# A fused attention, mixture of experts and gated layer on one core: the tokens' numbers scattered at a later place, the constants and the attention in another order

## The chip, the cores and the metric

The kernel runs on one core of a Trainium2 chip. Its engines are PE (TensorE, matrix products), DVE (VectorE), ACT (ScalarE), POOL (GpSimd) and SP (SyncE, which here only issues DMAs). Each engine works through its own list of instructions in order; a semaphore makes an instruction wait for another engine or for a DMA. The metric is the time of one execution on the device in microseconds, and the lower is the better.

## The reference

Three layers follow one another. Attention with a memory term over B=2, H=8, S=576, D=64, then a top-1 mixture of 8 experts with a capacity of 288 tokens, then a gated layer of width 1536, all in float32:

```python
scores = np.where(causal, -1e9, scale * q @ k.T); a = softmax(scores); local = a @ v
mem_out = (phi(q) @ M_prev) / (phi(q) @ z_prev + 1e-6)        # phi(x) = where(x > 0, x, exp(x) - 1) + 1
x = g * mem_out + (1 - g) * local                              # 1152 tokens of 512
expert_idx = argmax(x @ w_gate); gate_w = softmax(x @ w_gate)[expert_idx]
# the first 288 tokens of each expert are kept, in the order of the tokens
y[e] = relu(x[e] @ w1[e]) @ w2[e];  out[i] = gate_w[i] * y[expert of i, place of i]   # 0 where not kept
result = ((out @ w_a) * (out @ w_b)) @ w_out
```

## The kernel before

**Attention.** The 16 heads make 8 pairs, n = 0 to 7, four to a batch. A pair's 576 rows are cut into five tiles; a tile of a pair is a unit. Per pair, q and k are loaded by SP, turned by PE, split into a high and a low part by ACT and DVE, and POOL and SP place copies of these parts side by side: POOL makes copies in `d` and `qz`, and SP issues two DMAs `d<-s` (`side_by_side`, L495, the issue is L500), without which the pair's scores can't start. Per unit, PE makes the scores (L579), DVE the masked minima, ACT the exponentials, PE turns them and multiplies by v. Per pair, POOL makes phi(q) (L475, L481), and PE multiplies it by the memory (L522).

**Gate.** As tiles of tokens become whole, PE turns them and multiplies by `w_gate` (L730, 8 columns), DVE finds each token's expert, its probability and its place. `gate5` (L816) then has POOL issue an indirect DMA that scatters 128 tokens of 512 numbers into a DRAM buffer `xs_d`, sorted by experts; there are ten of them, five for each batch. `rank` (L854) sorts the experts by their number of tokens; it and `gate4b` (L788, the places of the last three tiles) run on DVE at the attention's end.

**Zeros.** `init_dram` (L407) has SP write zeros into `xs_d` and into the output, in ten parts between the attention's other issues. Its part 0 also writes `far`, a number that means none, into the 1152 words of `id_d`, a DRAM buffer with one 4-byte number to a row. The zeros come from a tile that shares its memory with the tile h, so these DMAs are printed as `xs_d<-h` and `out_dram<-h`.

**Experts and the gated layer.** Each float32 weight is split into a high and a low part by ACT (L961) and DVE (L964), or by integer operations on DVE (L1353 to L1363) with ACT's help (L1349), and each product is made of three matmuls (L949 to L951). Weights come from DRAM in blocks of 1 MB into a few buffers (`raw`, `raws`, `rawd`), issued by SP (L935 for the experts, L972 for the gated layer) as soon as a buffer is free. PE turns the tokens of an expert (L958) and uses L1539 for one kind of expert product.

**Tokens' numbers.** The last layer's results are written back by an indirect scatter which needs, for each row in the sorted order, the number of its token. `token_ids` (L898) makes them: four DVE instructions (L899 to L902) give every token's place `dsi`, and ten indirect DMAs of POOL (L808, by `scatter`) write the tokens' numbers `tid` into `id_d`, each 128 words of 4 bytes; a tile of 64 rows writes 64. Afterwards POOL loads all of `id_d` into the tile `ids`. The first use of `ids` is the first scatter of the output.

**What sets the order.** Nothing in the list of an engine is sorted by hand. `Plan` (L111) is a list scheduler: every piece of work has an engine, a cost, what it comes after, the buffers that it takes, and a key. It takes the work that can start first and, among those that can start within a share `AHEAD_` of the cost, the one with the smallest key; the keys are the pair's or unit's number plus an offset from the table `KEYS`. A call of `there` tells the plan when a load is expected. A piece of work's costs and due times only decide the order in which instructions are written, never a wait on the chip. The class `Way` (L1277) plans the experts and the gated layer in the same manner, with keys in the unit of expected time.

Of the kernel before, what the change touches and what calls it, by code (L numbers as in the profile page):

```python
# [21 lines left out]
SVB = 3  # L22
KEYS = dict(E=-210.8, E_=-463.7, F=981.4, F_=15.6, L=-19.8, M=23.3, M_=-352.9, N=429.9, N_=-217.9, O=185.9, O_=61.1,
            P=293, P_=-109.5, S=-8.9, S_=374.1, T=-187.5, T_=-396.9, V=-472.6, V_=432.7, X=-6.7, X_=-271.4, cv=-185,
            d=-57.5, e1=-507.1, e2=213.4, ec=894.9, eh=-120.4, ep=-803.9, ex=-13.3, ey=107.1, g1=-624, g1_=436.1,
            g1b=25.7, g1b_=19, g2=-336.8, g2_=216.5, g2b=186.5, g2b_=-486.8, g3=71.5, g3_=-527.6, g4=-221.2,
            g4_=157.3, g4b=209.7, g4b_=-689.3, g5=6, ge=68.8, ge_=125, gw=407.6, gw_=-144.8, kh=-415.4, kl=-145,
            kt=-27.5, mm=-190.6, mm_=40.1, mn=45.7, mo=217.3, mo_=-200.5, pb=-229.7, pw=-257.8, px=-331.6, qd=-154.1,
            qe=38.2, qh=-186.8, ql=237.9, qm=-200.6, qp=-217.5, qr=630.5, qt=-193.9, tc=-222.5, tot=279.3, tr=0.6,
            w=280.2, w_=-166)  # L30
GK = 0.0
AHEAD_ = 0.094
CHANGE = 0.25
# [3 lines left out]
ZS = 1  # L37
STIR = [16, 0, 16, 0]
GROUPS = [(0, 2), (2, 5)]
# [157 lines left out]
def fused_kernel(  # L197
# [125 lines left out]
    if STACK:  # L323
        mask2 = ap1.tile([128, S], F32, name="mask2")
        nc.gpsimd.memset(mask2, 0.0)
        for h in range(2):
            nc.gpsimd.affine_select(out=mask2[64 * h:64 * h + 64], in_=mask2[64 * h:64 * h + 64], pattern=[[-1, S]],
                                    base=NF_ * 128, channel_multiplier=1, compare_op=ALU.is_ge, fill=BIG)


        qd = [ap1.tile([128, 128], F32R, name=f"qd{n}") for n in range(3)]
        for t in qd:
            nc.gpsimd.memset(t.bitcast(F32), 0.0)
    for n in (1, 0):
# [7 lines left out]
    for t in range(2):  # L342
        nc.scalar.dma_start(out=zr[:, t, :], in_=z_prev.rearrange("b h d -> (b h) d"))
    Mp = M_prev.rearrange("b (p t) d e -> t d (b p) e", t=2)
    for t in range(2):
        nc.sync.dma_start(out=mb[64 * t:64 * t + 64, :, 64 * t:64 * t + 64], in_=Mp[t])

    bet = cst.tile([128, H], F32, name="bet")
    nc.scalar.dma_start(out=bet, in_=beta.rearrange("(o h) -> o h", o=1).to_broadcast([128, H]))
    load(0, "v")  # L350
    load(1)
    rg = cst.tile([128, H], F32, name="rg")
    rog = cst.tile([128, H], F32, name="rog")
# [32 lines left out]
    def gate_constants():  # L386
        nc.gpsimd.affine_select(out=tri, in_=ones, pattern=[[1, 128]], base=-1, channel_multiplier=-1,
                                compare_op=ALU.is_ge, fill=0.0)
        nc.gpsimd.iota(up, pattern=[[1, E]], base=0, channel_multiplier=0, allow_small_or_imprecise_dtypes=True)
        for p in range(E):  # L390
            nc.gpsimd.memset(prm[:, p:p + 1], float(RANKS[p]))
            nc.gpsimd.memset(lim[:, p:p + 1], float(LIMITS[p]))
        nc.gpsimd.iota(rev, pattern=[[-1, E]], base=E, channel_multiplier=0, allow_small_or_imprecise_dtypes=True)
        nc.gpsimd.affine_select(out=low, in_=ones[:, 0:E * E].rearrange("p (a b) -> p a b", a=E),
                                pattern=[[1, E], [-1, E]], base=-1, channel_multiplier=0,
                                compare_op=ALU.is_ge, fill=0.0)
        for b in range(B):
            nc.gpsimd.iota(tid[:, b * NT:b * NT + NT], pattern=[[128, NT]], base=b * S, channel_multiplier=1)
        for t in (oh, lgs, accs, gvm, pos, over, zero):
            nc.gpsimd.memset(t, 0.0)  # L400
# [601 lines left out]
    def dve_(c):  # L1002
        return 0.07 + 1.05e-3 * c

    for n in range(min(2, len(pairs))):
        for j, w in enumerate("qkv"):
            there(("load", n, w), [(w, (w, n))], (4.5, 5.5, 10.0, 11.0, 12.0, 13.0)[3 * n + j])
    there("d0", [("d", ("d", 0))])
    there("zr", late=9.0)
    work("small", "PE", 0.2, small_constants, ["zr"], (-6, None), [("C", "small")], late=0.4)  # L1010
    ZP = 10
    for n, (b, p) in enumerate(pairs):
        at_ = n * UP
        if n > 1:
            for w in "qkv":
# [9 lines left out]
             [("qT", n), ("s", n)])  # L1025
        work(("qd", n), "POOL", 1.1, lambda n=n: q_stack(n), [("ql", n)], (at_, "qd"), [("qd", ("qd", n))], [("s", n)])
        work(("qm", n), "POOL", 1.616, lambda n=n: q_min(n), [("qe", n)], (at_, "qm"), (), [("eq", n)])
        work(("qp", n), "POOL", 1.45, lambda n=n: q_phi(n), [("qm", n), ("qr", n)], (at_, "qp"), (),
# [7 lines left out]
        if n:  # L1036
            work(("dq", n), "POOL", 2.75, lambda n=n: q_beside(n), [("qh", n)], (at_, "d"), [("d", ("d", n))], [("s", n)])
            work(("dk", n), "POOL", 1.36, lambda n=n: k_beside(n), [("kh", n), ("dq", n)], (at_, "d"), (),
# [9 lines left out]
        for i in UNITS:  # L1048
# [6 lines left out]
            for h in range(1 if one else 2):  # L1055
                work(("M", u, h), "DVE", dve_(W), lambda u=u, h=h: minima(u, h), [("S", u)], (at_, "M"),
                     [("sv", ("sv", u, h))], [u])
# [32 lines left out]
    for z in range(ZP):  # L1090
        work(("z", z), "SP", 2.2, lambda z=z: init_dram(z, ZP), [("S", units[ZU + z * ZS])], (999, None), late=2.0)
    L0 = NTT - NT
    for b in range(B):
# [3 lines left out]
        for i in range(NT):  # L1097
# [6 lines left out]
            work(("g2", t), "PE", 0.92, lambda t=t: gate2(t), [("g1b", t)], (at_, "g2"), [("C", ("g2", t))], [("xt", t)])  # L1104
            work(("g2b", t), "DVE", 0.075, lambda t=t: gate2b(t), [("g2", t)], (at_, "g2b"), [], [("g2", t)])
        prev = [("g3", (0, NT))] if last else []
        for g, (i0, i1) in enumerate(G):
# [10 lines left out]
            for j, t in enumerate(range(*T)):  # L1118
                eng = "DVE" if not last or t - L0 in WDVE else "ACT"
                work(("w", t), eng, 0.61 if eng == "ACT" else 0.4, lambda t=t, eng=eng: weigh(t, eng),  # L1120
                     [("gw", T), ("g1", t)], (at_, "w"))
                work(("g5", t), "POOL", 1.04, lambda t=t, T=T: gate5(t, *T), [("g4b", T), ("w", t)] +
                     [("z", z) for z in range(ZP)], (at_, "g5"), late=2.3)
# [96 lines left out]
    if FAST:  # L1220
# [17 lines left out]
        def tokens_ahead():  # L1238
# [8 lines left out]
             ["prex"] + [("pre", j) for j in range(NF)] + [("wa", n) for n in range(2 * WA0)])  # L1247
    gate_constants()
    sched.run()
# [27 lines left out]
    class Way:  # L1277
# [329 lines left out]
        def forward(self, W, key, t, before):  # L1607
# [240 lines left out]
```

## Time and profile before

| | |
|---|---|
| median of 3 runs | 450.18 us (445.99 to 450.95) |
| the profiled execution | 448.67 us, of which the span of the trace is 446.9 us |
| mean granted clock of TensorE | 0.963 of full speed |
| busy share of PE, DVE, ACT, POOL | 90%, 59%, 46%, 23% |

PE is the engine with the most work. Its idle time and the stretches at a lower granted clock are therefore the first things to look at, and then what ended them. A busy share says nothing on an engine that waits for another at the one place and holds it up at the other.

### The profile page before, as it was taken

To read this page: it belongs to the slowest core of one execution; us is meant where nothing else is said; L and a number is where in the kernel's file an instruction comes from. 1 tells how busy PE (TensorE), PEld (TensorE's weight loads), DVE (VectorE), ACT (ScalarE), POOL (GpSimd) and SP (SyncE) were. 2 spreads that over 40 slices of the span, in tenths; PEclk is the share of its full clock that TensorE was granted. 3 is DMA by queue.
4 is the path that set the end of the run, shared out by engine and by line. 5 is a ranking of instruction groups with operands and counts; after the bars stand their busy time and mean duration, and the time that the engine had idled before them with its cause. 6 is when DMAs were issued, how large, how long until landed. Compare 5 with 4: busy or idle time off the path is not lost.

```text
span 446.9 us, 7876 instructions
## 1 busy us (share of the span) xinstructions
PE 402.1 (90%) x2868; PEld 351.3 (79%) x2868; DVE 264.5 (59%) x639; ACT 207.1 (46%) x451; POOL 104.8 (23%) x182
## 2 busy tenths in 40 slices
PE   6789998989799999588759997999999999999993
PEld 6677887967687999477749795889778897778892
DVE  4567775689784675263350014989885859933231
ACT  3767887479785541351250214444635345113010
POOL 8684576057700005126000000000000000000302
PEclk9999999899899969699869999999999999999998
DMA  3679999838980006399898999965530000000101
GB/s 75 150 171 129 248 289 313 189 72 280 238 294 6 1 2 227 96 392 212 184 366 306 345 390 407 407 243 189 165 118 1 0 1 1 0 1 0 73 25 60
DMA packets 59912, 74.48 MB, mean 167 GB/s; under 512 B 33955, under 2 KB 33955, under 8 KB 59856
## 3 DMA queue, kind: packets, MB, share of 16 engines
q1 hardware_dynamic: 58016, 70.48, 52.0%
q0 software_dynamic: 1632, 3.31, 2.2%
q8 instruction: 27, 0.44, 0.4%
q14 instruction: 29, 0.24, 0.2%
q10 hardware_dynamic: 208, 0.01, 0.0%
HBM read 58.75 MB, written 11.64 MB: 158 GB/s over the span
## 4 chain that ended last, share of the span: by engine, by line
PE 37%; DMA 13%; issue 4%; POOL 1%; ACT 1%; DVE 1%; SPq 0%; POOLq 0%
DMA raw<-in_moe_w_dram 11%; PE bank L949 8%; PE bank L950 8%; PE bank L951 8%; PE bank L1677 4%; PE bank L1678 4%; PE bank L1679 4%; DMA rawd<-xs_d 2%; PE bank L1539 1%; POOL out_dram L808 1%; DVE part L964 1%; ACT part L961 0%; PE bank L958 0%; DVE h L1461 0%; PE bank L1548 0%
## 5 line engine op out<-in xcount | busy, mean ns | idle before, releaser
L949 PE MATMUL bank<-x,part 128*128 128x512 f32 (+1 forms) x192 | 66.7, 348 | 0.4 <-ACT x L961 0.4
L950 PE MATMUL bank<-x,part 128*128 128x512 f32 (+1 forms) x192 | 66.6, 347 | 0.0
L808 POOL DMA_INDIRECT out_dram<-c,ids x4 | 3.9, 986 | 195.6 <-DVE c L1687 193.8
L615 ACT ACTIVATE a<-sv,mn 128x128 f32<-128x128 f32 (+4 forms) x72 | 41.9, 584 | 13.9 <-DVE mn L595 12.9
L949 PEld LDWEIGHTS bank<-x,part 128*128 128x128 f32 x192 | 36.1, 188 | 5.0 <-issue 0.6
L950 PEld LDWEIGHTS bank<-x,part 128*128 128x128 f32 x192 | 36.1, 188 | 4.2
L595 DVE CUSTOM_DVE_ANT_0 sv<-psS,mask 128x128 f32<-128x128 f32 (+4 forms) x72 | 34.6, 515 | 7.9 <-PE psS L579 6.2
L630 PE MATMUL psB<-ident,a 128*128 128x128 f32 x200 | 31.7, 285 | 2.0 <-ACT a L615 1.6
L951 PE MATMUL bank<-x,part 128*128 128x512 f32 (+1 forms) x96 | 33.4, 347 | 0.0
L951 PE MATMUL bank<-x,xt 128*128 128x512 f32 (+1 forms) x96 | 33.3, 346 | 0.0
L630 PEld LDWEIGHTS psB<-ident,a 128*128 128x128 f32 x200 | 24.2, 146 | 6.3 <-ACT a L615 3.4
L647 ACT COPY at<-psB 128x512 f32<-128x512 f32 (+2 forms) x48 | 23.8, 512 | 11.1 <-PE psB L630 10.3
L964 DVE TENSOR_TENSOR x<-bank,x 128x160 f32 (+3 forms) x12 | 4.1, 366 | 39.6 <-ACT x L961 39.6
L961 ACT CAST part<-u 128x1024 fp32r<-128x1024 f32 x18 | 18.7, 1050 | 19.1 <-DVE u L1363 15.8
L1653 ACT COPY c<-bank 128x512 f32<-128x512 f32 (+1 forms) x24 | 11.8, 499 | 25.7 <-PE bank L951 21.5
L1656 DVE TENSOR_TENSOR c<-c,bank 128x512 f32<-128x512 f32 (+1 forms) x24 | 13.7, 576 | 16.0 <-PE bank L951 11.0
L961 ACT CAST a<-c 128x512 fp32r<-128x512 f32 (+1 forms) x12 | 6.4, 534 | 35.4 <-DVE c L1656 28.8
L961 ACT CAST part<-raw 128x1024 fp32r<-128x1024 f32 x14 | 14.2, 1049 | 18.0 <-DMA raw<-in_moe_w_dram 18.0
L964 DVE TENSOR_TENSOR part<-raw,part 128x1024 fp32r<-128x1024 f32 x12 | 14.5, 1229 | 11.7 <-ACT part L961 11.7
L808 POOL DMA_INDIRECT xs_d<-x,di x10 | 10.6, 1060 | 40.8 <-DVE ggt L769 35.0
L951 PEld LDWEIGHTS bank<-x,xt 128*128 128x128 f32 x96 | 18.0, 188 | 2.1
L951 PEld LDWEIGHTS bank<-x,part 128*128 128x128 f32 x96 | 18.0, 188 | 2.1
(281 smaller groups left out, 1090.4 us busy)
## 6 DMA issues: line engine op xcount, KB each, us to landing
raw<-in_moe_w_dram SPq DMA_DIRECT2D x16, 1024.0 KB, 8.8
raws<-in_moe_w_dram SPq DMA_DIRECT2D x6, 1024.0 KB, 15.0
rawd<-in_moe_w_dram SPq DMA_DIRECT2D x6, 1024.0 KB, 20.8
xs_d<-h SPq DMA_DIRECT2D x10, 512.0 KB, 4.7
raw<-in_moe_w_b_dram SPq DMA_DIRECT2D x4, 1024.0 KB, 13.9
d<-s SPq DMA_DIRECT2D x14, 288.0 KB, 3.9
rawd<-in_moe_w_a_dram SPq DMA_DIRECT2D x3, 1024.0 KB, 18.9
raws<-in_moe_w_out_dram SPq DMA_DIRECT2D x3, 1024.0 KB, 5.3
```

What stands on the lines that cost most here:

```text
L595: nc.vector.tensor_tensor_reduce(out=o, in0=i0, in1=i1, scale=1.0, scalar=3.0e38, op0=ALU.add, op1=ALU.min, accum_out=mn[:M])
L615: nc.scalar.activation(out=st[u, "a"][:M, h, 0:W], in_=sv[:M, 0:W], func=AF.Exp, scale=-1.0, bias=mn[:M], **more)
L630: nc.tensor.transpose(pt[:kr, M * j:M * j + M], a_t[:M, h, 128 * kt:128 * kt + kr], ident[:M, :M])
L647: eng(out=st[n, a, "at"][:, h0:h0 + nh, 0:i + 1, c0:c0 + 128], in_=pt[:, 0:m * 128].rearrange("p (h k m) -> p h k m", h=nh, m=128))
L808: ins = nc.gpsimd.indirect_dma_start(out=out_[:, :], out_offset=bass.IndirectOffsetOnAxis(ap=idx, axis=0), in_=in_, in_offset=None, bounds ...
L949: nc.tensor.matmul(out_, lhsT=wh, rhs=xh, start=first, stop=False)
L950: nc.tensor.matmul(out_, lhsT=wh, rhs=xl, start=False, stop=False)
L951: nc.tensor.matmul(out_, lhsT=wl, rhs=xh, start=False, stop=last)
L961: nc.scalar.copy(out=to, in_=src)
L964: (eng or nc.vector).tensor_tensor(out=to, in0=src, in1=hi, op=ALU.subtract)
L1677: nc.tensor.matmul(o, lhsT=g[:, 0, ts_], rhs=wh[:, m, :], start=m == 0, stop=False)
L1678: nc.tensor.matmul(o, lhsT=g[:, 0, ts_], rhs=wl[:, m, :], start=False, stop=False)
```

## The change

- **Tokens' numbers.** The work `ids` (`token_ids` and the load of `ids`) is no longer planned ahead of the gated layer but behind the pieces that load the gated layer's last block of `w_out`, with a later key. It is the plan's order that knows of these loads; no semaphore is added.
- **Start.** The load of `M_prev` is issued behind the second pair's loads instead of ahead of the first pair's v. POOL's constants become pieces of planned work: the mask and the zeros of the stacked last tile (`last`, with a smaller mask), the zeros in `qz` (`pad1`, `pad0`), the gate's constants (`consts`). The tile of zeros is set by DVE. `stir`, matmuls on zeros that give PE something to do at the start, has 8 instead of 16 in its second place.
- **Order.** New `KEYS`, `AHEAD_` .132 instead of .094, due times of the first loads, and three costs.

```diff
-KEYS = dict(E=-210.8, E_=-463.7, F=981.4, F_=15.6, L=-19.8, M=23.3, M_=-352.9, N=429.9, N_=-217.9, O=185.9, O_=61.1,
...
+KEYS = dict(E=502, E_=221, F=-302.1, F_=64, L=118.7, M=-967.5, M_=566.5, N=-316.3, N_=50.2, O=-50.5, O_=-139, P=675.4,
...
-AHEAD_ = 0.094
+AHEAD_ = 0.132
...
-STIR = [16, 0, 16, 0]
+STIR = [16, 0, 8, 0]
...
+    nc.vector.memset(zero, 0.0)
...
-        nc.gpsimd.memset(mask2, 0.0)
...
+    def last_tile_constants():
+        nc.gpsimd.memset(mask2[:, 0:NF_ * 128], 0.0)
         for h in range(2):
...
+            c = slice(NF_ * 128, S)
+            nc.gpsimd.affine_select(out=mask2[64 * h:64 * h + 64, c], in_=zero[64 * h:64 * h + 64, 0:64], pattern=[[-1, 64]],
+                                    base=0, channel_multiplier=1, compare_op=ALU.is_ge, fill=BIG)
...
-    for n in (1, 0):
+    def padding(n):
         for h in range(2):
             nc.gpsimd.memset(qz[n][64 - 64 * h:128 - 64 * h, S * h:S * h + S].bitcast(F32), 0.0)
...
-    Mp = M_prev.rearrange("b (p t) d e -> t d (b p) e", t=2)
-    for t in range(2):
-        nc.sync.dma_start(out=mb[64 * t:64 * t + 64, :, 64 * t:64 * t + 64], in_=Mp[t])
...
     load(0, "v")
     load(1)
+    Mp = M_prev.rearrange("b (p t) d e -> t d (b p) e", t=2)
+    for t in range(2):
+        nc.sync.dma_start(out=mb[64 * t:64 * t + 64, :, 64 * t:64 * t + 64], in_=Mp[t])
...
-        for t in (oh, lgs, accs, gvm, pos, over, zero):
+        for t in (oh, lgs, accs, gvm, pos, over):
...
-            there(("load", n, w), [(w, (w, n))], (4.5, 5.5, 10.0, 11.0, 12.0, 13.0)[3 * n + j])
+            there(("load", n, w), [(w, (w, n))], (5.2, 7.9, 8.5, 9.5, 10.5, 11.5)[3 * n + j])
...
+    work("at first", "POOL", 5.5, lambda: None, (), (-99, None))
+    for name, cost, do in (("last", 1.9, last_tile_constants), ("pad1", 1.2, lambda: padding(1)),
+                           ("pad0", 1.2, lambda: padding(0)), ("consts", 3.6, gate_constants)):
+        work(name, "POOL", cost, do, ["at first"], (0, name))
...
-        work(("z", z), "SP", 2.2, lambda z=z: init_dram(z, ZP), [("S", units[ZU + z * ZS])], (999, None), late=2.0)
+        work(("z", z), "SP", 2.2, lambda z=z: init_dram(z, ZP), [("S", units[ZU + z * ZS]), "consts"], (999, None), late=2.0)
...
-    gate_constants()
...
-            self.work("ids", "POOL", 14.0, tell, (), t - 20, late=3.0)
...
+                if i == NI3 - 1:
+
+                    self.work("ids", "POOL", 14.0, tell, [("ld", O, n) for n in range(2)], t, late=3.0)
```

**Where the four instructions of `token_ids` stand on DVE.** A row is a line of the kernel, an operation and its tiles (`u` is a buffer of the integer split, `raws`, `rawd` and `raw` are blocks of weights, `part` a half of a weight that is split, `c` a product being summed). Before, in the middle of an early expert:

```order
L1359 SCALAR_TENSOR_TENSOR u_4555<-raws_1917,u_4555 128x1024
L964 TENSOR_TENSOR part_210<-raw_4557,part_4602 128x1024 x2
L899 TENSOR_TENSOR big<-oh,rs 128x80
L900 TENSOR_REDUCE dst<-big 128x10
L901 TENSOR_TENSOR dst<-dst,pos 128x10
L902 TENSOR_TENSOR dsi<-dst,over 128x10
L1363 SCALAR_TENSOR_TENSOR u_4555<-raws_1917,u_4555 128x1024
L1359 SCALAR_TENSOR_TENSOR u_4556<-rawd_1977,u_4556 128x1024
```

After, in the split of one of the gated layer's last blocks; the lines have moved by five to ten (L904 to L907 are the old L899 to L902, L1361 and L1363 the old L1353 and L1355):

```order
L1666 TENSOR_TENSOR c<-c,bank_2598 128x304
L1361 TENSOR_SCALAR u_4548<-u_4548 128x1024
L1363 TENSOR_SCALAR u_4548<-u_4548 128x1024
L904 TENSOR_TENSOR big<-oh,rs 128x80
L905 TENSOR_REDUCE dst<-big 128x10
L906 TENSOR_TENSOR dst<-dst,pos 128x10
L907 TENSOR_TENSOR dsi<-dst,over 128x10
L1361 TENSOR_SCALAR u_4547<-u_4547 128x1024
L1363 TENSOR_SCALAR u_4547<-u_4547 128x1024
L1367 SCALAR_TENSOR_TENSOR u_4547<-raw_196,u_4547 128x1024
```

The four have moved past some 90 rows of DVE's list, and the ten scatters with them, which wait for the last of the four; POOL's own list has nothing else there.

**Where the write of `far` stands on SP.** `d_76<-s_74` is the copy of the third pair, n = 2; `ldk` and `ldv` are loads of later pairs' k and v. Before:

```order
L281 DMA ldk_80<-in_k_dram 128x4x64 x2
L284 DMA ldk_80<-in_k_dram 64x2x64
L500 DMA d_76<-s_74 64x1152 x2
L412 DMA xs_d<-h_97 128x2x512
L417 DMA id_d<-far 128x9x1
L281 DMA ldv_82<-in_v_dram 128x4x64 x2
```

After, with L417, L422 and L505 for the old L412, L417 and L500:

```order
L281 DMA ldk_80<-in_k_dram 128x4x64 x2
L284 DMA ldk_80<-in_k_dram 64x2x64
L417 DMA xs_d<-h_97 128x2x512
L422 DMA id_d<-far 128x9x1
L505 DMA d_76<-s_74 64x1152 x2
L281 DMA ldv_82<-in_v_dram 128x4x64 x2
```

The copy that the third pair's scores need is now issued behind the first part of the zeros and behind the 1152 words of `far`.

**Where the first batch's five scatters of tokens stand on POOL.** `d_77<-s_75` and `qz_99<-s_75` are the last pair's copies (n = 7), without which its scores can't start. Before:

```order
L517 COPY d_76<-s_74 64x576 x2
L808 DMA xs_d<-x_95,di 2560x512 x5
L612 MEMSET a 128x64
L508 COPY d_77<-s_75 64x576 x2
L509 COPY qz_99<-s_75 64x576
L510 COPY qz_99<-s_75 64x512
L512 COPY qz_99<-s_75 64x64
L475 TENSOR_SCALAR eq<-eq 128x576
```

After, with L513 to L522 for the old L508 to L517, L813 for L808 and L480 for L475:

```order
L617 MEMSET a 128x64
L513 COPY d_77<-s_75 64x576 x2
L514 COPY qz_99<-s_75 64x576
L515 COPY qz_99<-s_75 64x512
L517 COPY qz_99<-s_75 64x64
L522 COPY d_77<-s_75 64x576 x2
L813 DMA xs_d<-x_95,di 2560x512 x5
L480 TENSOR_SCALAR eq<-eq 128x576
L485 MEMSET ph 128x64
```

The last pair's copies now stand ahead of the five scatters, and its phi (from the old L475 on) behind them.

At the attention's end, the lists of PE and DVE have `gate4b` and its matmuls ahead of `rank` where they had them behind it. The first batch's matmuls of the gate (the old L730) now stand in groups of 8, 4, 4 and 4 among other work where there were 4 and 16. From the experts on, the lists of PE, ACT and SP have the same rows in the same order as before.

## Rows read from the trace of the kernel before

**Rows 1.** Stretches (us): length, busy of each engine (xinstructions), PEclk, DMA share, GB/s.
```profile
190.00:204.00 14.00, 12.27 (x97) 10.25 (x96) 10.62 (x16) 7.44 (x18) 5.05 (x5) 1.00 1.05 392
204.00:222.00 18.00, 13.98 (x91) 13.34 (x91) 4.65 (x7) 3.56 (x7) 6.33 (x6) 0.91 0.96 155
222.00:276.00 54.00, 44.24 (x614) 39.37 (x613) 10.33 (x20) 14.76 (x42) 1.07 (x1) 0.94 0.98 360
276.00:440.00 164.00, 164.00 (x826) 138.22 (x824) 111.53 (x141) 60.94 (x87) 5.88 (x6) 1.00 0.25 94
```

**Rows 2.** Timeline of POOL, first and last scatter into id_d: start, us, instruction, [idle before <-releaser].
```profile
197.73 1.72 POOL L808 DMA_INDIRECT id_d<-tid,dsi  x1 [15.96 <-DVE dsi L902]
...
212.31 0.91 POOL L808 DMA_INDIRECT id_d<-tid,dsi  x1 [1.06 <-DMA id_d<-tid,dsi]
```

**Rows 3.** Chain that ended last, three pieces between 176 and 276: start, us, what.
```profile
199.49 24.38 DMA raw<-in_moe_w_dram
...
229.84 3.25 PE bank L1539 x64
...
272.83 1.11 PE bank L1539 x32
```

**Rows 4.** Stretches during and after the writes of id_d<-far.
```profile
38.00:46.00 8.00, 7.24 (x64) 5.86 (x63) 4.81 (x16) 7.02 (x16) 2.69 (x5) 1.00 0.93 72
47.00:50.00 3.00, 3.00 (x23) 2.78 (x22) 2.83 (x12) 2.01 (x9) 2.94 (x5) 1.00 1.05 364
```

**Rows 5.** Timeline of SP, its issues around id_d<-far, and the last weight loads.
```profile
32.68 1.18 SPq L500 DMA_DIRECT2D d<-s  x2
...
34.95 1.39 SPq L417 DMA_DIRECT2D id_d<-far  x1
...
314.31 0.37 SPq L972 DMA_DIRECT2D raw<-in_moe_w_b_dram  x1
...
325.74 0.37 SPq L972 DMA_DIRECT2D raws<-in_moe_w_out_dram  x1
```

**Rows 6.** Timeline of ACT, the last use of those loads.
```profile
342.28 1.15 ACT L1349 ACTIVATE u<-raws 128x1024 f32<-128x1024 f32 x1
```

**Rows 7.** Stretch of the last weight loads.
```profile
280.00:330.00 50.00, 50.00 (x257) 42.74 (x256) 46.13 (x56) 24.92 (x34) 0.00 (x0) 1.00 0.66 246
```

**Rows 8.** Timeline of PE in the attention, five of its rows.
```profile
6.96 2.31 PE L309 MATMUL psC<-qz 128*128 128x256 f32 x16 [0.47 <-POOL qz L336]
...
45.35 0.48 PE L579 MATMUL psS<-d 128*128 128x256 f32 x2
...
74.47 0.39 PE L579 MATMUL psS<-d 128*128 128x256 f32 x1 [0.88 <-DMA d<-s]
...
120.05 1.23 PE L522 MATMUL psS<-mb,ph 128*128 128x130 f32 x4 [2.38 <-DVE sums L673]
...
185.02 1.94 PE L958 MATMUL bank<-ident,raws 128*128 128x128 f32 x8 [5.58 <-DMA raws<-xs_d]
```

**Rows 9.** Timeline of POOL, last batch's work behind the xs_d scatters.
```profile
113.45 0.67 POOL L508 CAST d<-s 64x576 fp32r<-64x576 f32 x1 [2.80 <-DMA xs_d<-x,di]
...
172.93 0.97 POOL L808 DMA_INDIRECT xs_d<-x,di  x1 [3.30 <-DVE rt L877]
```

**Rows 10.** Three stretches of half clock in the attention.
```profile
86.00:90.00 4.00, 4.00 (x20) 3.51 (x19) 2.77 (x13) 2.13 (x5) 0.15 (x1) 0.60 0.47 76
120.00:124.00 4.00, 3.95 (x20) 3.95 (x21) 1.50 (x8) 0.74 (x2) 1.87 (x5) 0.59 0.93 186
180.00:188.00 8.00, 2.98 (x13) 3.01 (x14) 1.31 (x3) 3.00 (x6) 1.28 (x2) 0.58 0.24 77
```

**Rows 11.** Timeline of DVE: first of rank, first of g4b, and the later place of token_ids.
```profile
169.39 0.17 DVE L857 SCALAR_TENSOR_TENSOR rs<-psC,rev 128x8 f32<-128x8 f32 x1 [1.99 <-PE psC L835]
...
171.23 0.16 DVE L795 TENSOR_SCALAR gp<-gvm 128x3 f32<-128x3 f32 x1
...
310.30 0.69 DVE L1353 TENSOR_SCALAR u<-u 128x1024 f32<-128x1024 f32 x1
```

More of the change, by code (lines that the diff above doesn't have):

```diff
@@ L22 @@
 SVB = 3
-KEYS = dict(E=-210.8, E_=-463.7, F=981.4, F_=15.6, L=-19.8, M=23.3, M_=-352.9, N=429.9, N_=-217.9, O=185.9, O_=61.1,
[L24 to L30, printed above, removed]
+KEYS = dict(E=502, E_=221, F=-302.1, F_=64, L=118.7, M=-967.5, M_=566.5, N=-316.3, N_=50.2, O=-50.5, O_=-139, P=675.4,
+            P_=-121.7, S=327, S_=188.6, T=-56.2, T_=-185.4, V=-77.6, V_=-123.1, X=-248.6, X_=66.4, consts=613.8,
+            cv=-172.7, d=-43.2, e1=-207.9, e2=269, ec=1026.2, eh=-418.9, ep=113.4, ex=-759.2, ey=332.5, g1=274.3,
+            g1_=-394.9, g1b=-306.3, g1b_=-110.1, g2=67.8, g2_=-153, g2b=51.5, g2b_=-136.7, g3=-413.3, g3_=-237.4,
+            g4=-39.8, g4_=118, g4b=-451.8, g4b_=-214.9, g5=18.9, ge=-74.6, ge_=-163.6, gw=687.7, gw_=40.6, kh=-4.2,
+            kl=149.6, kt=-65.6, last=69.9, mm=-247.7, mm_=1082, mn=-147.5, mo=188.3, mo_=401, pad0=-71.5, pad1=18.1,
+            pb=101.2, pw=3.2, px=-43.8, qd=64.4, qe=-113.3, qh=-114.8, ql=-307.9, qm=31.9, qp=-222.9, qr=158.8,
+            qt=-196.2, tc=219.1, tot=410.5, tr=-407.9, w=221.9, w_=92.1)
 GK = 0.0
-AHEAD_ = 0.094
+AHEAD_ = 0.132
 CHANGE = 0.25
@@ L324, in fused_kernel @@
         mask2 = ap1.tile([128, S], F32, name="mask2")
-        nc.gpsimd.memset(mask2, 0.0)
+        qd = [ap1.tile([128, 128], F32R, name=f"qd{n}") for n in range(3)]
+    def last_tile_constants():
+        nc.gpsimd.memset(mask2[:, 0:NF_ * 128], 0.0)
         for h in range(2):
-            nc.gpsimd.affine_select(out=mask2[64 * h:64 * h + 64], in_=mask2[64 * h:64 * h + 64], pattern=[[-1, S]],
-                                    base=NF_ * 128, channel_multiplier=1, compare_op=ALU.is_ge, fill=BIG)
-        qd = [ap1.tile([128, 128], F32R, name=f"qd{n}") for n in range(3)]
+            c = slice(NF_ * 128, S)
+            nc.gpsimd.affine_select(out=mask2[64 * h:64 * h + 64, c], in_=zero[64 * h:64 * h + 64, 0:64], pattern=[[-1, 64]],
+                                    base=0, channel_multiplier=1, compare_op=ALU.is_ge, fill=BIG)
         for t in qd:
             nc.gpsimd.memset(t.bitcast(F32), 0.0)
-    for n in (1, 0):
+    def padding(n):
         for h in range(2):
@@ L1025, in fused_kernel @@
              [("qT", n), ("s", n)])
-        work(("qd", n), "POOL", 1.1, lambda n=n: q_stack(n), [("ql", n)], (at_, "qd"), [("qd", ("qd", n))], [("s", n)])
-        work(("qm", n), "POOL", 1.616, lambda n=n: q_min(n), [("qe", n)], (at_, "qm"), (), [("eq", n)])
+        work(("qd", n), "POOL", 1.1, lambda n=n: q_stack(n), [("ql", n), "last"], (at_, "qd"), [("qd", ("qd", n))], [("s", n)])
+        work(("qm", n), "POOL", 1.75, lambda n=n: q_min(n), [("qe", n)], (at_, "qm"), (), [("eq", n)])
         work(("qp", n), "POOL", 1.45, lambda n=n: q_phi(n), [("qm", n), ("qr", n)], (at_, "qp"), (),
@@ L1036, in fused_kernel @@
         if n:
-            work(("dq", n), "POOL", 2.75, lambda n=n: q_beside(n), [("qh", n)], (at_, "d"), [("d", ("d", n))], [("s", n)])
+            work(("dq", n), "POOL", 2.75, lambda n=n: q_beside(n), [("qh", n), "pad0", "pad1"], (at_, "d"), [("d", ("d", n))], [("s", n)])
             work(("dk", n), "POOL", 1.36, lambda n=n: k_beside(n), [("kh", n), ("dq", n)], (at_, "d"), (),
@@ L1055, in fused_kernel @@
             for h in range(1 if one else 2):
-                work(("M", u, h), "DVE", dve_(W), lambda u=u, h=h: minima(u, h), [("S", u)], (at_, "M"),
+                work(("M", u, h), "DVE", dve_(W), lambda u=u, h=h: minima(u, h), [("S", u)] + (["last"] if one else []), (at_, "M"),
                      [("sv", ("sv", u, h))], [u])
@@ L1104, in fused_kernel @@
             work(("g2", t), "PE", 0.92, lambda t=t: gate2(t), [("g1b", t)], (at_, "g2"), [("C", ("g2", t))], [("xt", t)])
-            work(("g2b", t), "DVE", 0.075, lambda t=t: gate2b(t), [("g2", t)], (at_, "g2b"), [], [("g2", t)])
+            work(("g2b", t), "DVE", 0.075, lambda t=t: gate2b(t), [("g2", t), "consts"], (at_, "g2b"), [], [("g2", t)])
         prev = [("g3", (0, NT))] if last else []
@@ L1121, in fused_kernel @@
                      [("gw", T), ("g1", t)], (at_, "w"))
-                work(("g5", t), "POOL", 1.04, lambda t=t, T=T: gate5(t, *T), [("g4b", T), ("w", t)] +
+                work(("g5", t), "POOL", 1.4, lambda t=t, T=T: gate5(t, *T), [("g4b", T), ("w", t)] +
                      [("z", z) for z in range(ZP)], (at_, "g5"), late=2.3)
```

## The prediction

> **What bounds the kernel now.** I read the profile in three steps. First the page's slices: PE is busy nearly throughout, with dips in the attention, a hole where the attention hands over to the experts, and a low stretch between 204 and 276 us. The stretches put numbers to it. From 276 to 440 us PE is busy for 164.00 of 164 us at full clock [rows 1]: nothing there can be shortened by an order, and whatever arrives earlier at its beginning moves the end by as much. So the change is worth what it takes out of the time before 276 us. Between 204 and 222 PE is idle for 4.0 us, between 222 and 276 for 9.8 us, 13.8 us together, and the DMA engines are busy all the time (share 0.96 and 0.98) [rows 1]. That is a stage bound by weights that come in.
>
> Second, what the DMA engines do there. Between 190 and 204 us they move 392 GB/s, between 204 and 222 us 155 GB/s, and from 222 on 360 GB/s, at the same busy share [rows 1]. Something keeps them busy without moving bytes. The ten scatters of tokens' numbers start at 197.73 and the last at 212.31 us [rows 2], and each sends 128 separate words of 4 bytes. The chain that ended last goes through this: a 1 MB weight block issued at 199.49 takes 24.38 us to land, PE's product L1539 waits for what is made of it until 229.84, and further such waits follow until 272.83, where the last of them ends [rows 3]. A second place speaks for the same cause: `far`, also 1152 words of 4 bytes, is issued at 34.95 [rows 5], and between 38 and 46 us the engines move 72 GB/s at a share of 0.93; 47 to 50 us show 364 GB/s [rows 4].
>
> Third, PE's waits in the attention and its clock [rows 8 to 10], which the new order may shorten.
>
> **The change, part by part.**
>
> *Scatters away from the experts' weights.* In 18 us (392 - 155) x 18 = 4,270 KB less were moved than at the rate ahead of it; at 392 GB/s that is 10.9 us of transfers [rows 1]. The stage waits for loads to its end, so this carries through to 272.83: **-10.9 us**. Ends: 0, if the rate fell for another reason, and -13.8, PE's whole idle time in the stage, since less than that can't be removed by loads alone. I take 10.9 because the loss of bytes is measured and the idle time is larger than it, so PE can use it. What is late next is the block after it: the buffers come free as PE goes, and a rest of 3 us of idle time stays.
>
> Here the Trainium skill, "DMA: Bandwidth & Descriptors", section "Anatomy of one DMA — SWDGE (gpsimd) path", speaks against the change: it gives a DMA from GpSimd about 2 us of fixed time, most of it the receipt of the last write, and beyond that bytes at 436 GB/s. By that rule ten scatters of 0.5 KB would take nothing of the other loads' rate, this term would be 0 and the time that of the second rival below; the trace's 155 and 72 GB/s beside such writes speak against it.
>
> *The scatters' new place.* The four DVE instructions now stand before the integer split that ran at 310.30 [rows 11], and the scatters follow at once. DVE is busy there for 46.13 of 50 us [rows 7], and four instructions of about 0.2 us (the small ones of [rows 11]) add 0.8 us to it; PE has parts in store, since it never idles, so 0. On the chip the scatters are not behind the last loads: of these, three are issued from 314.31 to 325.74 [rows 5], inside the 18 us that the writes would take. The last is used at 342.28 [rows 6], 16.5 us after its issue. If it took 24.38 us as the one of [rows 3], it would be 7.9 us late. Since the DMA engines have room there (share 0.66, [rows 7]) I take **0**, ends 0 and +7.9. The numbers themselves are needed only by the output's scatters, beyond 400 us; POOL does 5.88 us of work between 276 and 440 [rows 1].
>
> *Start.* `stir`'s 16 matmuls at 6.96 take 2.31 us and waited 0.47 us for POOL's zeros [rows 8]. Eight take 1.16, and the zeros are no longer made first: -1.6. Behind them stand k's turning, its split and the first scores. DVE gets five small instructions ahead of the split, at 0.17 to 0.2 us each [rows 11] some +0.9, of which a part lies beside the loads. I take **-1.0**, ends 0 and -1.6. POOL's constants lie beside the first pair's work, with no reader soon.
>
> *`far` ahead of the third pair's copy.* Before, the copy was issued at 32.68 and the zeros and `far` from 33.96 and 34.95 on [rows 5]; the scores that need the copy ran at 45.35 without a wait [rows 8]. Now the copy is queued behind 1152 small writes. By [rows 4] the slow stretch is over at 47 us, so a copy issued in it lands by then; the scores are due at 45.35 - 1.0, and PE works in order, so everything behind stands too. **+2.0**, ends 0 and +2.7. A later copy is no longer behind other zeros; the wait at 74.47 was 0.88 us [rows 8]: **-0.9**.
>
> *Clock after the gate's matmuls.* From 86 to 90 us the granted clock is 0.60 [rows 10], right behind the gate's 8-column matmuls, which the old order issues in a group of 16. At full clock that work takes 4.00 x 0.60, so 1.6 us are lost. These now come in groups of four to eight with wide matmuls between: **-1.6**, ends 0 and -1.6.
>
> *POOL's stall in the last batch.* PE waits 2.38 us at 120.05 [rows 8], because the last pair's copy at 113.45 waited 2.80 us on POOL behind the first batch's scatters of tokens [rows 9], and afterwards the clock is 0.59 for 4 us, 1.6 us lost [rows 10]. The copies now stand ahead of these scatters. **-2.4 and -1.6**, ends 0 and -4.0. Queued behind the scatters is now phi of the last pair, whose memory product stands late on PE.
>
> *Hand-over.* `rank` runs on DVE from 169.39 to 171.23, then `gate4b` [rows 11], then the scatter at 172.93 that waits for DVE [rows 9]. PE waits 5.58 us for the tokens loaded behind these scatters, at 185.02 [rows 8]. With `gate4b` first the scatters can go 1.84 us earlier: **-1.8**, ends 0 and -1.8. The order of experts, 1.8 us later, is wanted by the first weights only, which lie in wait when the tokens come.
>
> *All of the attention.* -1.0 + 2.0 - 0.9 - 1.6 - 4.0 - 1.8 = -7.3 us. The new order has gaps of its own that the old trace can't show. Of eight places like these a third may come back; I take +2.3, so **-5.0**, ends -9.3 (no stall for the copy and no gaps) and +4 (the old gaps stay in other places and the copy stalls).
>
> **Sum.** 448.67 - 10.9 - 5.0 = 432.8 us for an execution like the profiled one. That one lies 1.5 us under the median of the runs, so 434 us for the median. A measurement of this kernel can tell about 1% from no change, 4.5 us.
>
> **Rivals.**
>
> *The new order gives nothing.* The attention's waits come from chains between engines, and another order moves them more easily than it removes them. 0 to +4 instead of -5: 450.2 - 10.9 + 0 to 4 = 439 to 443 us. For it: most of the gaps are under 1 us, and the terms are sums of single places. Against: the two largest, at 120.05 and 185.02, have one cause each, which the order removes.
>
> *The low rate isn't the scatters'.* Blocks of weights with a different pattern could be slow by themselves between 204 and 222 us; then only -5 remains, 445 us. Against it: `far`'s stretch, where other loads are under way and the same thing happens.
>
> *The scatters' new place costs.* The move is an order, not a wait, so the writes meet the last three loads: +7.9 as worked out, 434 + 8 = 442 us, if PE has no stock of split weights.
>
> *Slower: the copy behind `far`.* If the third pair's copy fares like the weight block of [rows 3], 24.38 us from an issue at about 36, it lands at 60.4, and PE, in order, stands for 16 us from 44.4 on. It decides from a stall of 11 us, the scatters' gain. With the order's other gains lost behind it: 450.2 - 10.9 + 16 = 455 us. Against: in the old trace the rate was back at 47 us [rows 4].
>
> **How the numbers follow.** The forecast 0.60 (427 to 440 us: ends -13.8 and -9.3, or -8 and -2); the new order gives nothing 0.20; the low rate stays 0.08; the new place costs 0.07; slower by the copy 0.05. The range of 427 to 445 us takes in all but the last and half of the third. Under 445.7 us lie the forecast, nearly all of the first rival, most of the others: faster 0.90. Within 1%: 0.06, from the second rival with gaps of the new order. Slower 0.04.
>
> **What would show it.** In the changed kernel's stretches, no low rate at a high DMA share from 185 to 270 us; no load of 24 us there; PE full from about 260 instead of 276 us. A low rate instead at about 295 to 315 us, behind the scatters, with PE full beside it. PE's wait of 2.38 gone and the clock full behind it, no 0.60 after the gate's matmuls of the first batch; the wait for tokens at the hand-over under 4 us; a wait of 1 to 3 us of the third pair's scores for `d<-s`. I am wrong if the low rate stays among the experts' weights, if PE idles after 276, or if the waits in the attention add up to more than before.

## The result, and the profile after

The changed kernel takes **431.22 us** (median of 4 runs, 429.41 to 434.82), the kernel before beside it 448.86 us. The ratio is 0.962, with a 95% interval of 0.953 to 0.971: 3 to 5% faster. Here and below, a ratio is that of the fast runs alone, while a median is that of all runs, so the two can differ a little. The profiled execution took 430.72 us with a span of 428.9 us, 18.0 us less than before's. Beside each other on another chip the two gave 0.960 (0.953 to 0.966).

The stretches of the changed kernel, in the columns of [rows 1]:

```profile
190.00:204.00 14.00, 14.00 (x112) 12.43 (x111) 10.10 (x12) 8.04 (x19) 0.00 (x0) 1.00 1.05 387
204.00:222.00 18.00, 18.00 (x188) 17.64 (x187) 9.78 (x14) 9.33 (x18) 0.00 (x0) 1.00 1.05 386
222.00:256.00 34.00, 32.63 (x494) 29.09 (x493) 3.86 (x11) 7.08 (x26) 0.00 (x0) 1.00 0.98 363
257.00:421.00 164.00, 163.72 (x824) 138.65 (x825) 112.70 (x146) 61.85 (x88) 20.19 (x17) 1.00 0.33 100
```

Between 204 and 222 us the DMA engines move 386 GB/s at a share of 1.05, where [rows 1] have 155 at 0.96; PE is busy without a gap. The full stretch of 164 us, in which PE is busy for 163.72, begins at about 257 instead of 276 us.

In the chain that ended last (the run of work and waits, followed back from the end of the kernel), the waits for weight blocks have shrunk to one of 8.53 us, and the piece that stood at 272.83 in [rows 3] stands at 255.01:

```profile
229.29 8.53 DMA raw<-in_moe_w_dram
...
255.01 1.16 PE bank L1547 x32
```

POOL's timeline of the changed kernel shows where the scatters went, and the tokens' scatter of the hand-over, at 172.93 in [rows 9]:

```profile
169.34 0.97 POOL L813 DMA_INDIRECT xs_d<-x,di  x1 [1.55 <-DVE rt L864]
...
293.70 1.19 POOL L813 DMA_INDIRECT id_d<-tid,dsi  x1 [113.88 <-DVE dsi L907]
...
309.07 0.99 POOL L813 DMA_INDIRECT id_d<-tid,dsi  x1 [0.30 <-issue]
```

The attention did not become shorter in the way that was forecast. Stretches of the changed kernel: three places at which the clock was to be looked at, the low rate of `far`, and the scatters' new place:

```profile
10.00:20.00 10.00, 6.47 (x33) 6.03 (x33) 5.81 (x22) 3.68 (x13) 3.62 (x11) 0.66 0.62 137
80.00:90.00 10.00, 9.58 (x78) 9.05 (x78) 5.50 (x22) 7.00 (x20) 1.14 (x3) 1.00 0.83 251
120.00:130.00 10.00, 8.59 (x68) 6.75 (x67) 9.01 (x32) 8.96 (x25) 2.23 (x7) 1.00 0.93 310
38.00:46.00 8.00, 7.57 (x69) 6.30 (x66) 5.43 (x19) 5.74 (x14) 4.37 (x9) 1.00 1.10 48
294.00:304.00 10.00, 10.00 (x46) 8.13 (x45) 9.55 (x14) 5.34 (x9) 8.34 (x6) 1.00 0.42 22
```

The kernel before, for the first of them:

```profile
10.00:20.00 10.00, 7.14 (x53) 6.37 (x55) 6.38 (x27) 7.20 (x22) 5.62 (x18) 1.00 0.74 163
```

Half clock is gone behind the gate's matmuls (80 to 90 us) and in the last batch (120 to 130 us), as forecast from [rows 10]; it has come up at the start, 0.66 where it was 1.00. PE's timeline of the changed kernel shows its waits at the start, behind `far` and at the hand-over to the experts:

```profile
10.78 0.74 PE L584 MATMUL psS<-s,d 128*128 128x256 f32 x4 [2.72 <-ACT s L494]
...
14.17 2.08 PE L584 MATMUL psS<-s,d 128*128 128x256 f32 x8 [2.65 <-DVE s L498]
...
47.23 0.44 PE L673 MATMUL psC<-ident,os 128*128 128x128 f32 x2 [1.01 <-ACT os L667]
...
181.91 1.18 PE L963 MATMUL bank<-ident,raws 128*128 128x128 f32 x8 [4.43 <-DMA raws<-xs_d]
...
184.54 1.70 PE L1454 MATMUL bank<-d,raw 128*128 128x160 f32 x5 [1.45 <-ACT d L966]
```

Two waits of 2.72 and 2.65 us stand ahead of the first scores. DVE's timeline shows the second one's cause: the small constants' five instructions run ahead of the split of k that the scores need, and the first of them waits for ACT and takes 1.37 us itself.

```profile
10.87 1.37 DVE L367 TENSOR_SCALAR rg<-rg 128x8 f32<-128x8 f32 x1 [1.36 <-ACT rg L366]
...
13.35 0.76 DVE L498 TENSOR_TENSOR s<-psS,s 128x576 fp32r<-128x576 f32 x1
```

The wait of 1.01 us at 47.23 has `far` behind it. In the chain that ended last, the write of `far` stands for 11.42 us, and ACT's split of k, with the copy for which PE waits right behind it, starts when it ends:

```profile
34.85 11.42 DMA id_d<-far
46.27 0.63 ACT s L494
46.90 0.29 ACT os L667
47.23 0.44 PE psC L673 x2
```

### The profile page after: what moved, and what is told of

Its sections match the earlier page's. It is cut to its first block, busy times and chain, and to the rows that moved or that the text cites. A ratio compares the mean times of both kernels' runs of the same rounds, so it can differ in the third digit from the quotient of the medians.

```text
span 428.9 us, 7838 instructions
## 1 busy us (share of the span) xinstructions
PE 398.1 (93%) x2860; PEld 348.3 (81%) x2860; DVE 267.0 (62%) x640; ACT 206.8 (48%) x451; POOL 103.9 (24%) x181
## 4 chain that ended last, share of the span: by engine, by line
PE 64%; DVE 8%; POOL 8%; issue 7%; DMA 6%; ACT 4%; ACTq 0%; SPq 0%; POOLq 0%
PE bank L954 10%; PE bank L955 9%; PE bank L956 9%; PE bank L1687 4%; PE bank L1688 4%; PE bank L1689 4%; PE bank L1547 3%; DMA id_d<-far 3%; PE bank L1454 3%; PE psB L954 2%; DVE sv L600 2%; PE psB L956 2%; PE bank L1490 2%; PE psB L955 2%; DMA raw<-in_moe_w_dram 2%
## 5 line engine op out<-in xcount | busy, mean ns | idle before, releaser
L813 POOL DMA_INDIRECT id_d<-tid,dsi x10 | 13.6, 1362 | 116.6 <-DVE dsi L907 113.9
L1666 DVE TENSOR_TENSOR c<-c,bank 128x512 f32<-128x512 f32 (+1 forms) x24 | 13.8, 577 | 16.0 <-PE bank L956 11.0
L813 POOL DMA_INDIRECT out_dram<-c,ids x4 | 4.0, 988 | 80.8 <-DVE c L1697 79.0
L662 PE MATMUL psC<-at,ldv 128*64 128x256 f32 (+1 forms) x192 | 20.0, 350 | 0.5 <-ACT at L652 0.4
L813 POOL DMA_INDIRECT xs_d<-x,di x10 | 10.4, 1036 | 41.2 <-DVE ggt L774 37.0
## 6 DMA issues: line engine op xcount, KB each, us to landing
raw<-in_moe_w_b_dram SPq DMA_DIRECT2D x4, 1024.0 KB, 13.8
raws<-in_moe_w_out_dram SPq DMA_DIRECT2D x3, 1024.0 KB, 12.4
```

The lines of the kernel that those rows point to most:

```text
L662: nc.tensor.matmul(po[64 * h:64 * h + 64, c0:256], lhsT=vt[:, kt, h, 0:D], rhs=at_[:, h, kt, c0:256], start=kt == 0, stop=kt == 2 * a + 1)
L813: ins = nc.gpsimd.indirect_dma_start(out=out_[:, :], out_offset=bass.IndirectOffsetOnAxis(ap=idx, axis=0), in_=in_, in_offset=None, bounds ...
```

## The experiments

A number that most of the runs share is **the stage**: from PE's turning of the first sorted tokens (at 185.02 in [rows 8], 181.91 above) to the start of the last product that waits for a block (272.83 in [rows 3], 255.01 above). It leaves out what happened in the attention.

| kernel | stage, us | length |
|---|---|---|
| before | 185.02 to 272.83 | 87.8 |
| changed | 181.91 to 255.01 | 73.1 |
| changed, once more | 183.66 to 255.03 | 71.4 |
| scatters' move alone | 184.59 to 258.85 | 74.3 |
| scatters' move alone, once more | 187.12 to 262.79 | 75.7 |
| order and start alone | 185.81 to 272.22 | 86.4 |
| changed, no scatters | 186.98 to 260.89 | 73.9 |
| before, rows of 64 bytes | 189.08 to 261.71 | 72.6 |
| before, rows of 512 bytes | 187.56 to 263.88 | 76.3 |
| before, scatters twice | 187.63 to 297.27 | 109.6 |

The stage's start tells of the attention, in one execution of each run: in the six with the old order it lies between 184.59 and 189.08 us, 186.8 in the mean, in the four with the new one between 181.91 and 186.98, 184.6 in the mean.

### The scatters' move alone

```diff
-            self.work("ids", "POOL", 14.0, tell, (), t - 20, late=3.0)
...
+                if i == NI3 - 1:
+                    self.work("ids", "POOL", 14.0, tell, [("ld", O, n) for n in range(2)], t, late=3.0)
```

> The kernel before with one part of the change: the tokens' numbers are scattered behind the last block of w_out, the rest as before. Theory (the ten scatters of 4-byte words are what keeps the rate low, and the loads' loss is carried through to the end): 432 to 437 us, nearly the whole of the change, no rate under 350 GB/s beside a DMA share near 1 between 190 and 270 us, PE full from about 261 us. Rival (the scatters give no more than the 10.9 us of the term, the rest of the change is the attention's order): 438 us. Rival (the low rate belongs to the weight blocks): 447 us or more, with the low rate still at 204 to 222 us.

436.25 us against 450.11 of the kernel before on the same chip, ratio 0.977 (0.957 to 0.998). Its stretch of 204 to 222 us:

```profile
204.00:222.00 18.00, 15.98 (x173) 15.55 (x172) 10.10 (x14) 9.88 (x19) 0.00 (x0) 1.00 1.05 387
```

The low rate is gone, and the stage is 13.5 us shorter than before's. The theory holds, and the rival with the weight blocks falls. The ratio's interval is too wide to decide between 11 and 15 us; the run once more, below, has 12 to 19 us, which speaks against the rival that gave the scatters 10.9 us only.

### Order and start alone

The changed kernel with the two edits above taken back.

> The changed kernel with the tokens' numbers back at their old place; the start and the attention's order stay changed. Theory: the attention's order gives 2 to 4 us, so 444 to 448 us, and the low rate is back between about 200 and 220 us. Rival (order 5 us or more, scatters 11): 442 us or less. Rival (the two parts depend on each other): the gains of this one and of the scatters alone, against the kernel before, don't add up to that of the whole change within 3 us.

447.72 us, ratio 0.999 (0.995 to 1.003): no gain that can be told from none, -0.5 us with an interval of -2.4 to +1.4. The low rate is back:

```profile
204.00:222.00 18.00, 13.67 (x88) 12.41 (x85) 5.15 (x8) 4.01 (x8) 6.73 (x6) 0.81 1.05 157
```

By the ratios this 0.5 us and the scatters' 15.7 (in the run once more, below) make 16.2 us, beside 17.0 for the whole change in the first measurement and 18.3 in the second: the two parts add up within the 3 us that were asked for.

### Both once more, beside each other

> The changed kernel once more, beside the scatters alone on the same chip. Theory (the attention's order is worth less than 5 us, and the start's loss of 2.8 us is why): 430 to 435 us, 0 to 4 us under the run with the scatters alone. Rival (the order is worth the 5 us forecast): 5 us or more under it.

> The kernel before with the scatters' move alone, once more, beside the changed kernel on the same chip. Theory: 433 to 437 us; from PE's first product of the sorted tokens to the last wait for a weight block some 74 us as in the changed kernel, 88 in the kernel before. Rival (the order is worth 5 us or more): 437 us or more.

432.92 us (ratio 0.960) and 437.62 us (0.965, 0.958 to 0.973), before 451.91. By the ratios the order and the start are worth 0.6%, 2.6 us, on top of the scatters' move. The medians lie 4.7 us apart, more than my 0 to 4 and less than the rival's 5, and 437.62 lies just in the rival's range. The two intervals overlap: nothing and the forecast 5 us are both possible.

### The changed kernel without the scatters

```diff
-        for t in range(NTT):
-            M = rows[t % NT]
-            scatter("id" + key, id_d, dsi[:M, t:t + 1], tid[:M, t:t + 1], N)
```

> The changed kernel without the ten scatters of tokens' numbers; the buffer then holds no token's number and the last scatters of the output write no row, so the end behind PE's last matmul is not to be compared. Theory (the new place costs nothing): PE's last matmul ends within 1 us of the changed kernel's, the loads behind 293 us run at full rate and land in 4 to 6 us. Rival (the new place costs a part of the gain): PE's last matmul 2 to 8 us earlier.

Its hand-over came later in this execution, so PE's end is compared from the last product behind the stage. In the chain and PE's timeline of the changed kernel:

```profile
256.51 0.34 PE bank L1556
```

```profile
421.81 0.40 PE L1689 MATMUL bank<-part,h 128*48 128x512 f32 x1
```

and of the one without scatters:

```profile
262.41 0.34 PE bank L1553
```

```profile
427.70 0.40 PE L1686 MATMUL bank<-part,h 128*48 128x512 f32 x1
```

165.3 us in both. At their new place the scatters cost PE nothing, though the DMA engines move 22 GB/s between 294 and 304 us (above). The three last loads of weights, issued at 297.34, 302.65 and 307.97 us, do land late in the changed kernel, after 10.7, 13.9 and 12.4 us (the last two took 4.8 and about 5.3 before). The last one's 12.4 us is inside the 16.5 us that the prediction gave it until its use, and PE doesn't wait. This is the theory's result; the trace of the run without scatters gives no landing times, so that number of the expectation stays open.

### Rows of 64 and of 512 bytes, and the scatters twice

In the first two a buffer of wider rows takes the scatters of the kernel before, at the old place, with a constant as the content (`k` is 16 or 128 words). The tokens' numbers are left out, so the output's scatters write no row:

```diff
+    idw_d = drm.tile([NI * 128, k], I32, name="idw_d")
...
-            scatter("id" + key, id_d, dsi[:M, t:t + 1], tid[:M, t:t + 1], N)
+            scatter("id" + key, idw_d, dsi[:M, t:t + 1], ident[:M, 0:k].bitcast(I32), N)
```

> The kernel before with ten scatters at the old place that send 128 rows of 64 bytes each to another buffer instead of 128 words of 4 bytes (rows of a constant; the tokens' numbers are not written, so the output's last scatters write no row). Theory (each write that is shorter than some length costs about the same time on a DMA engine): the low rate stays as it was, under 200 GB/s over some 18 us. Rival (only words of 4 bytes, less than a line of memory, are slow): no low rate, PE full from about 261 us.

> As the run with 64 bytes, with rows of 512 bytes: the same count of descriptors, 128 times the bytes of the kernel before's. Theory (short writes are slow): no low rate, or under a quarter of the 10.9 us; PE full from 261 to 264 us. Rival (the slow thing is an indirect DMA of POOL, whatever its rows): the low rate stays between 204 and 222 us.

> The kernel before with the ten scatters at the old place issued twice, the second time into another buffer. Theory (a price for each short write): the low rate lasts about twice as long, 30 to 38 us, and PE is full 10 to 15 us later than before, the time 459 to 464 us. Rival (a fixed stall while scatters and loads meet, whatever their count): 450 to 453 us.

For the third, the line with `scatter` is followed by a second one into a buffer of its own. The stretch beside the scatters with rows of 64 bytes, of 512 bytes, and the long one with words of 4 bytes sent twice:

```profile
204.00:222.00 18.00, 17.18 (x140) 15.59 (x140) 12.98 (x19) 11.20 (x21) 10.71 (x10) 1.00 1.07 374
```

```profile
204.00:222.00 18.00, 15.41 (x102) 13.82 (x99) 8.55 (x12) 7.56 (x14) 6.87 (x7) 0.91 1.06 373
```

```profile
208.00:256.00 48.00, 18.15 (x134) 16.38 (x132) 10.57 (x15) 9.87 (x19) 16.15 (x16) 0.70 0.91 115
```

The count of descriptors is the same in the first two as before, and the rate stays at 374 and 373 GB/s, the stage at 72.6 and 76.3 us (one run each, 437.4 and 439.57 us beside 452.82 of the kernel before). So neither the indirect DMA nor its count of descriptors is slow: the **words of 4 bytes** are. My theory that every short write has its price falls at 64 bytes; where the limit lies between 4 and 64 bytes was not tried. Wider rows also lie further apart in DRAM, so these runs don't tell whether it is a write's length or the closeness of its neighbours that counts. Twice as many words make the low rate last about 48 us and the stage 21.8 us longer, more than the first ten cost (87.8 less 71.4 to 75.7), and one load stands in the chain with 47.79 us:

```profile
208.40 47.79 DMA rawd<-in_moe_w_dram
```

474.16 us beside 452.82 of the kernel before: the rival of a fixed stall falls, and my 459 to 464 us were too low. The rule of the Trainium skill that the prediction weighed ("DMA: Bandwidth & Descriptors", "Anatomy of one DMA — SWDGE (gpsimd) path"), by which such scatters take next to nothing, agrees with the rows of 64 and 512 bytes (374 and 373 GB/s) and not with the words of 4 (155).

### `far` as runs of 36 bytes

```diff
-            nc.sync.dma_start(out=id_d.rearrange("(t p) o -> p (t o)", p=128), in_=far)
+            nc.sync.dma_start(out=id_d.rearrange("(p t) o -> p (t o)", p=128), in_=far)
```

All words are the same number, so the order of them doesn't matter.

> The changed kernel with the 1152 words of far written as one run of 36 bytes from each of 128 partitions instead of as 1152 separate words; all words are the same number, so what is written stays the same. Theory (the count of small writes makes the low rate): the stretch of 38 to 46 us, at 48 GB/s before, comes back above 200 GB/s within 2 to 3 us, the third pair's copy lands in under 6 us instead of 11.6; the end moves little, 0 to 2 us earlier, since PE has other work in that stretch. Rival (any write to this buffer stalls the queues, whatever its count): the stretch stays under 100 GB/s for 6 us or more.

> The changed kernel with far written as 128 runs of 36 bytes, once more with more rounds. Theory (the words of far hold up the loads behind them by 4 to 5 us, and PE's wait at 47 to 50 us with them, by another amount in each execution): 1 to 3 us under the changed kernel on the same chip, and a narrower spread. Rival (later waits take it back): the same within 1 us.

The first time 433.81 us with an interval of 0.930 to 0.991, too wide to say anything. The second time 430.45 us (428.27 to 431.78) beside the changed kernel's 432.92 (430.51 to 437.22), ratios 0.953 and 0.960: about 2.5 us earlier in the medians, with intervals that overlap. What it does is plain in the trace of the second: the stretch that has 48 GB/s above has

```profile
38.00:46.00 8.00, 7.57 (x67) 6.70 (x67) 6.56 (x23) 7.31 (x18) 4.41 (x9) 1.00 0.89 238
```

and the third pair's copy, issued between 34 and 44 us, lands after 11.6 us in the changed kernel and after 4.6 us in this one (the view of the tile `d`):

```profile
DMA to landing us min/median/max: 11.6/11.6/11.6
```

```profile
DMA to landing us min/median/max: 4.6/4.6/4.6
```

The traces tell whether this is a price of `far` in either order or one of the copy's place behind it. PE's work between 40 and 60 us in the kernel before, in the changed one and in this one:

```profile
40.00:60.00 20.00, 19.05 (x162) 16.15 (x160) 13.26 (x47) 17.05 (x44) 10.98 (x19) 1.00 0.98 204
40.00:60.00 20.00, 16.92 (x135) 14.05 (x135) 14.16 (x50) 14.27 (x38) 8.59 (x13) 1.00 0.93 181
40.00:60.00 20.00, 18.51 (x152) 15.59 (x152) 15.29 (x55) 16.01 (x42) 10.16 (x18) 1.00 0.89 259
```

In five executions the new order has `far` as words, and PE works 16.25 to 16.92 of these 20 us; it waits 1.01 to 3.09 us, for ACT behind `far` or for `d<-s`. In the three with `far` in runs it works 18.51 to 18.86 us and that wait is gone. In six with the old order and words it works 17.34 to 19.28 us, and only one has a wait of that size there (1.84).

### The start

> The changed kernel with the small constants of beta and z expected one microsecond later by the plan, which puts their five DVE instructions behind the first pair's split of k instead of ahead of it; no other engine's order changes. Theory (the start lost 2.8 us to these five instructions, PE's 2.65 us of idle time ahead of the first scores at 14.17 us, and half clock behind it): first full scores near 11.5 us, 1.5 to 3 us earlier at the end, 428 to 430 us. Rival (the start is hidden behind later waits for loads): the first scores earlier, the end the same within 0.5 us.

```diff
-    there("zr", late=9.0)
+    there("zr", late=10.0)
```

434.15 us, ratio 0.971 (0.958 to 0.984): no gain over the changed kernel's 0.962 and 0.960, as the rival had it, though the interval is too wide to tell half a microsecond. PE's timeline of this kernel:

```profile
11.22 2.12 PE L584 MATMUL psS<-s,d 128*128 128x256 f32 x12 [3.12 <-ACT s L494]
16.20 2.50 PE L527 MATMUL psS<-mb,ph 128*128 128x130 f32 x10 [2.86 <-DMA mb<-in_M_prev_dram]
```

The scores come at 11.22 without a second wait, and then the memory product waits 2.86 us for `M_prev`, whose load the change had put behind the second pair's. The last run has the constants later, this load ahead of the second pair's, and `far` in runs:

```diff
     load(0, "v")
+    Mp = M_prev.rearrange("b (p t) d e -> t d (b p) e", t=2)
+    for t in range(2):
+        nc.sync.dma_start(out=mb[64 * t:64 * t + 64, :, 64 * t:64 * t + 64], in_=Mp[t])
     load(1)
```

> The changed kernel with far in 128 runs, the small constants behind the first split of k, and the load of M_prev ahead of the second pair's loads. Theory (the start's chain was the five instructions and, behind them, the landing of M_prev, 2.86 us in the run with the constants alone): first full scores near 11.2 us, first memory product near 13.5 us instead of 16.0; with far 2 to 5 us under the changed kernel, 427 to 430 us. Rival (the chains of the new order, made for the late start, wait elsewhere): the same as with far alone within 1 us.

**428.97 us** (425.52 to 429.70), ratio 0.949 (0.943 to 0.956), 1.0% under the changed kernel on the same chip. PE's timeline of it:

```profile
10.87 2.42 PE L584 MATMUL psS<-s,d 128*128 128x256 f32 x12 [2.78 <-ACT s L494]
14.06 2.50 PE L527 MATMUL psS<-mb,ph 128*128 128x130 f32 x10 [0.77 <-POOL qd L336]
```

The memory product starts 2 us earlier than in the run before it. Against `far` alone it is 1.5 us, within what these runs can't tell.

## Why the prediction was right

The time (434, measured 431.22) and the direction were right, and so was the main mechanism: the low rate went with the scatters. The two terms of the sum were not: one was too small and the other too large, and the errors offset one another. That the sum came out so near is luck in that part.

- **Scatters away from the experts' weights**: mechanism right, term mis-sized. It was -10.9 us; the stage shows -13.5 and -12.1 us for the move alone and -14.7 and -16.4 for the whole change. The stage of the kernel before and of the changed one, as stretches, shows where the rest lies:

```profile
185.02:272.83 87.81, 73.12 (x787) 66.19 (x788) 28.20 (x45) 27.24 (x69) 12.45 (x11) 0.92 0.94 304
181.91:255.01 73.10, 70.28 (x786) 64.64 (x787) 26.77 (x39) 28.25 (x70) 0.00 (x0) 0.95 0.97 357
```

PE's idle time in the stage fell from 14.69 to 2.82 us, by 11.9, close to the term, and the forecast rest of 3 us of idle time is there. PE's busy time for the same products fell by 2.8 us as well, at a granted clock of 0.95 instead of 0.92; that the prediction had at nothing. In three more executions with the scatters moved (the changed kernel once more, the move alone twice) PE's idle time is 1.64 to 4.84 us and its busy time 69.42 to 71.38. The upper end of -13.8, PE's idle time, was no bound, since it left out the clock.
- **The scatters' new place** at 0: right, and the rival of +7.9 us fell with the run without scatters. It had given the last load 24.38 us; the load took 12.4. DVE's four instructions showed no cost either.
- **Start** at -1.0: wrong in sign. The first full scores came at 14.17 us; before, PE's first scores began at 11.34 us. The step that failed is the five instructions at 0.17 to 0.2 us: their first waits for ACT and takes 1.37 us. The clock of 0.66 there is not explained: it is still 0.66 in the last run, which has only the first of the two waits, and whether the eight matmuls fewer of `stir` have a part in it was not tried.
- **`far` ahead of the third pair's copy** at +2.0: right. The copy landed late, after 11.6 us, and PE works some 2 us less between 40 and 60 us where `far` goes as words ahead of it than where it goes as runs. The wait of 0.88 us at 74.47, at -0.9, is gone too.
- **Clock after the gate's matmuls** (-1.6) and **POOL's stall in the last batch** (-2.4 and -1.6): right, both stretches are at full clock and the wait of 2.38 us is gone. New waits of 0.83 and 0.74 us stand near it. The half clock is not the order's alone, though: between 80 and 100 us six executions of the old order have 0.83 to 1.00, eight of the new 0.91 to 1.00. PE's wait of 2.0 to 3.2 us near 120 us is in five of the six and in none of the eight.
- **Hand-over** at -1.8: less, and not under the 4 us that were forecast. The scatter behind `gate4b` moved from 172.93 to 169.34, but PE's wait went from 5.58 to 4.43 us only, and a new wait of 1.45 us for ACT stands behind it in this execution. Over all traces PE waits 5.53 to 7.48 us with the old order and 4.33 to 6.18 with the new.
- **All of the attention** at -5.0: too large, -0.5 (-2.4 to +1.4) by itself and some -2.6 with the scatters moved, though there the runs don't exclude 5. The start is the term that failed most, 2.8 us later instead of 1.0 earlier; with it the sum of -7.3 becomes -3.5, so that the allowance of 2.3 us for gaps was used up by one place. How much of these 2.8 us reaches the end isn't shown. Of the rivals, that the new order gives nothing came nearest for this part, with -5.0 for it outside what the run alone allows.

## What to carry to other kernels

Look in the trace for a stretch with a DMA share near 1 and few bytes, and ask which small writes were issued right ahead of it: their cost is not only on their own queue but on the large loads beside them. Scatter rows of 64 bytes instead of words of 4, write a constant as runs, or place such writes where no load is waited for; the first keeps the order as it was, but was tried here with a constant as the content only, without reading the numbers back. A new order of work that is tightly chained is worth what the runs show and not the sum of the gaps that it removes: here what the removed gaps gave came back in part as two waits and half clock at the start, and as a wait behind `far`.

## What the hardware showed that was not expected

Words of 4 bytes hold up all 16 DMA engines: ten scatters of up to 128 words cost 10.9 us of transfers (worked out from 155 against 392 GB/s over 18 us), 64-byte rows in the same count nothing that could be seen (374 GB/s). A 1 MB load issued among twenty such scatters took 47.79 us. The start showed a DVE instruction on 8 columns that took 1.37 us where others of its kind took 0.2. It took 0.82 to 1.38 us in all eight executions with the new start and 0.17 before; what held it stays open.
